# Moving GpSimd's weight sums away from the ends of third pairs, and VectorE's sums of h one step later

## The chip, the cores and the metric

The kernel runs on one core of a Trainium2 chip. The metric is the device time of one launch in microseconds (us). Every run named here is of one core; the profiled ones are all of the state "fast". Times of one kernel scatter by several us (before: 862.7 to 876.5 us over all groups of runs), so each comparison uses the runs of the kernel before that were made in the same rounds on the same chip. A ratio is the mean time of one kernel's fast runs over that of the other's fast runs of the same rounds; it is therefore not quite the ratio of the medians that are quoted beside it. One run of before in the last group (876.0 us) was marked slow and is in no ratio.

Engines in the profile: PE is TensorE (matmuls), PEld its weight loads, DVE is VectorE, ACT ScalarE, POOL GpSimd, SP SyncE. In this program the sums' operands and results lie in the memory called SBUF, TensorE's products in the one called PSUM. L207 is line 207 of the kernel. The changed kernel has nine more lines at that point, so L207 of before is L216 after.

## The reference, cut to what matters

An attention stage makes x (3072 tokens, 512 columns). Then eight experts are added up, each weighted by a routing table P that eight rounds of row and column normalisation make:

```python
for e in range(E):                         # E = 8
    h = np.maximum(x @ w1[e], 0.0)         # 512 -> 1024
    ye = h @ w2[e]                         # 1024 -> 512
    out += P[:, e:e + 1] * ye
```

## The kernel before

For experts 1 to 7 both products are done by a Strassen-like scheme with seven block products instead of eight. It needs sums and differences of quarters of all operands. Those of the weights (w1, w2) are made by GpSimd, those of h and of x by VectorE. A work item is one expert and one block of 768 tokens: there are 28. Step n of the program weaves TensorE's first product of item n (`hidden`, H) with the second product of item n-1 (`mixed`, C).

GpSimd's sums, four for each weight matrix of an expert, come from a generator of which one part runs at the end of each pair of token groups (a block has six groups of 128 tokens, taken in three pairs, i = 0, 1, 2):

```python
def quarters_of_w(e):
    ...
    pin(nc.gpsimd.tensor_tensor(s[:, 0], a21, a22, op=Alu.add))           # L139
    yield
    pin(nc.gpsimd.tensor_tensor(a21, a11, a21, op=Alu.subtract))          # L141
    yield
    pin(nc.gpsimd.tensor_tensor(s[:, 1], s[:, 0], a11, op=Alu.subtract))  # L143
    yield
    pin(nc.gpsimd.tensor_tensor(s[:, 2], a12, s[:, 1], op=Alu.subtract))  # L145
    ...
# quarters_of_w2: the same for w2, L155, L157, L159, L161

def next_weights():
    for e in range(2, E):
        for which in (1, 2):
            for half in range(2):
                load_w(e, which, pin=True, half=half)
                yield
            if which == 1:
                yield
        for g in (quarters_of_w(e), quarters_of_w2(e)):
            for n in range(4):
                next(g, None)
                if g.__name__ == "quarters_of_w" or n < 3:
                    yield
    ...
coming = next_weights()
```

VectorE's sums of h for one pair, and the places where both are called:

```python
def sums_of_h(e, b, i):
    ...
    pin(nc.vector.tensor_tensor(s_[:, 0], h21, h22, op=Alu.add))           # L206
    pin(nc.vector.tensor_tensor(s_[:, 1], s_[:, 0], h11, op=Alu.subtract)) # L207
    pin(nc.vector.tensor_tensor(h21, h11, h21, op=Alu.subtract))           # L208
    pin(nc.vector.tensor_tensor(s_[:, 2], h12, s_[:, 1], op=Alu.subtract)) # L209

ORDERS = (("a1", "d", "a2", "y", "a3", "a4", "t"), ("a1", "y", "a2", "a3", "d", "a4", "t"),
          ("a1", "a2", "y", "a3", "d", "a4", "t"))
# in mixed(e, b), for each pair i:
    for g, name in enumerate(ORDERS[i]):
        step(name)                              # one block product and its eviction
        if g == 3 and i + 1 < J // 2:
            sums_of_h(e, b, i + 1)
        if g == 6:
            if not last:
                pin(nc.gpsimd.dma_start(out=acc[:, b, i], in_=vt, accum_op=Alu.add))   # L276
            if e == E - 1 and not last:
                for j in (i, J // 2 + i):
                    pin((nc.gpsimd if final else nc.sync).dma_start(out=outv[b, j], in_=...))  # L279
            next(coming)
        ...
        yield 433

def woven(n):
    h = hidden(*work[n]) if n < len(work) else iter(())
    c = mixed(*work[n - 1]) if n else combine(B - 1)
    if n:
        sums_of_h(*work[n - 1], 0)              # the first pair's sums, at once
    ...
    parts = quarters_of_x(n + 1) if n + 1 < B else iter(())   # VectorE, only in the first blocks
    if n == 0:
        for _ in range(3):
            next(coming)
    for g, which in enumerate(plan):
        if g in (10, 19, 28, 37):
            next(parts, None)
        yield next(h if which == "H" else c)
```

So an expert has 12 places (4 blocks of 3 pairs) in which GpSimd gets one item: four loads and a pause take five, the sums the other seven, and the eighth sum shares the place of the next expert's first load. Three of the eight sums of each expert fall on the end of a third pair. Right there, `woven` asks VectorE for the next block's first sums of h.

The softmax here doesn't subtract the row's maximum and nothing guards it: scores larger than these inputs give would overflow.

Of the kernel before, what the change touches and what calls it, by code (L numbers as in the profile page):

```python
# [19 lines left out]
def kernel(  # L20
# [15 lines left out]
    E = moe_w_gate.shape[1]  # L36
# [7 lines left out]
    J = S // P  # L44
# [17 lines left out]
    def pin(ins):  # L62
        tc.keep_in_program_order(ins)
        return ins
# [41 lines left out]
    def load_w(e, which, pin=False, half=None):  # L106
        if half == 1:
            t = weights[e, which]
            src = (moe_w1[e].rearrange("(do di) f -> di do f", di=P) if which == 1
                   else moe_w2[e].rearrange("(fo fi) d -> fi fo d", fi=P))  # L110
        elif which == 1:
            t = wpool.tile([P, DO, F], F16, tag="w1")
            src = moe_w1[e].rearrange("(do di) f -> di do f", di=P)
        else:
            t = wpool.tile([P, FO, DD], F16, tag="w2")
            src = moe_w2[e].rearrange("(fo fi) d -> fi fo d", fi=P)
        part = slice(0, t.shape[1]) if half is None else slice(half * t.shape[1] // 2, (half + 1) * t.shape[1] // 2)
        ins = nc.gpsimd.dma_start(out=t[:, part], in_=src[:, part])
        if pin:
            tc.keep_in_program_order(ins)  # L120
        weights[e, which] = t
# [4 lines left out]
    def sums_of(b, j):  # L126
        if j < J // 2:
            return acc[:, b, j, 0:2, :]
        return acc[:, b, j - J // 2, 2:4, :]

    def quarters_of_w(e):

        if (e, 1) not in weights:
            load_w(e, 1, pin=True)
        t = weights[e, 1]
        lo, hi = slice(0, F // 2), slice(F // 2, F)
        a11, a12, a21, a22 = t[:, 0:2, lo], t[:, 2:4, lo], t[:, 0:2, hi], t[:, 2:4, hi]
        s = spool.tile([P, 3, 2, F // 2], F16, tag="s1")
# [7 lines that stand above are left out]
        weights[e, "q"] = dict(a11=a11, a12=a12, a22=a22, s1=s[:, 0], s2=s[:, 1], s3=a21, s4=s[:, 2])  # L146
# [16 lines left out]

    def next_weights():

        for e in range(2, E):
            for which in (1, 2):
                for half in range(2):
                    load_w(e, which, pin=True, half=half)
                    yield  # L170
                if which == 1:
                    yield
            for g in (quarters_of_w(e), quarters_of_w2(e)):
                for n in range(4):
                    next(g, None)
                    if g.__name__ == "quarters_of_w" or n < 3:
                        yield
        while True:
            yield

    coming = next_weights()

    def combine(b):
# [27 lines left out]
    def mixed(e, b):  # L211

        wq = weights[e, "t"]
        pw = pw_[-1]
        final = e == E - 1 and b == B - 1
        for i in range(J // 2):  # L216
            hq = hsums[e, b, i]
            last = final and i == J // 2 - 1
            plo, phi = pw[:, b * J + i, e:e + 1], pw[:, b * J + J // 2 + i, e:e + 1]
            if e == 1:  # L220
                for j in (i, J // 2 + i):
                    pin(nc.scalar.activation(out=sums_of(b, j), in_=sums_of(b, j), func=Act.Copy,
                                             scale=pw[:, b * J + j, 0:1]))
            a = yps.tile([P, DD // 2], F32, tag="y", name="a")
            d1 = yps.tile([P, DD // 2], F32, tag="y", name="d1")
            y2 = y2ps.tile([P, DD // 2], F32, tag="y", name="y2")
            vt = vkeep.tile([P, 4, DD // 2], F32, tag="v", name="vt")

            def prod(dst, hn, wn, first):
                for fo in range(FH):  # L230
                    pin(nc.tensor.matmul(dst, hq[hn][:, fo, :], wq[wn][:, fo, :], start=first and fo == 0,  # L231
                                         stop=fo == FH - 1, skip_group_check=True))

            def keep(k, p):
                if last and k == 1:
                    gather(k, a, p)
                    return
                pin(nc.scalar.activation(out=vt[:, k], in_=a, func=Act.Copy, scale=p))  # L238
                if last:
                    dst = acc[:, b, i, k, :]  # L240
                    pin(nc.vector.tensor_tensor(dst, dst, vt[:, k], op=Alu.add))

            def gather(k, src, p):
                dst = acc[:, b, i, k, :]
                pin(nc.vector.scalar_tensor_tensor(out=dst, in0=src, scalar=p, in1=dst, op0=Alu.mult, op1=Alu.add))  # L245

            def step(name):
                if name == "a1":
                    prod(a, "h11", "b11", True)
                    keep(0, plo)  # L250
                elif name == "a2":
                    prod(a, "s2", "t2", False)
                    keep(2, phi)
                elif name == "a3":
                    prod(a, "s1", "t1", False)
                    keep(3, phi)
                elif name == "a4":
                    prod(a, "s4", "b22", False)
                    keep(1, plo)
                elif name == "d":  # L260
                    prod(d1, "h12", "b21", True)
                    gather(0, d1, plo)
                elif name == "y":
                    prod(y2, "s3", "t3", True)
                    gather(3, y2, phi)
                else:
                    prod(y2, "h22", "t4", False)
                    gather(2, y2, phi)

            for g, name in enumerate(ORDERS[i]):  # L270
                step(name)
                if g == 3 and i + 1 < J // 2:
                    sums_of_h(e, b, i + 1)
                if g == 6:
                    if not last:
# [3 lines that stand above are left out]
                            pin((nc.gpsimd if final else nc.sync).dma_start(  # L279
                                out=outv[b, j], in_=sums_of(b, j).rearrange("p c d -> p (c d)")))  # L280
                    next(coming)
                if last and g >= 4:
                    for j, c, k, eng in {4: ((J // 2 + i, 1, 3, nc.sync), (i, 0, 0, nc.sync)),
                                         5: ((i, 1, 1, nc.scalar),), 6: ((J // 2 + i, 0, 2, nc.sync),)}[g]:
                        pin(eng.dma_start(out=outv[b, j][:, :, c * (DD // 2):(c + 1) * (DD // 2)],
                                          in_=acc[:, b, i, k, :]))
                yield 433
# [258 lines left out]
    for u in range(len(units) + 1):  # L546
        if u < len(units):
            n, h, kt = units[u]
            b, g = groups[n]
            i = u % per  # L550
# [146 lines left out]
# [4 lines that stand above are left out]
            sums_of_h(*work[n - 1], 0)  # L701
        if n == 0:
            plan = "".join("HC" if i % 7 else "H" for i in range(28))
        elif n < len(work):
            plan = "HHCHCHCHCCH" + 3 * "HHCHCHCHCHCH" + "CH"
        else:
            plan = 21 * "C"
        parts = quarters_of_x(n + 1) if n + 1 < B else iter(())
        if n == 0:
            for _ in range(3):  # L710
                next(coming)
        for g, which in enumerate(plan):
            if g in (10, 19, 28, 37):
                next(parts, None)
            yield next(h if which == "H" else c)
        assert next(h, None) is None and next(c, None) is None

    work = [(e, b) for e in range(1, E) for b in range(B)]

    def plain():  # L720
        yield from first_hidden(B - 1)
        yield from combine(B - 2)
        yield from woven(0)
# [47 lines left out]
```

## Time and profile before

| | before |
|---|---|
| median of its first three runs | 868.35 us (864.68 to 876.54) |
| span of the profiled run | 866.8 us |
| TensorE busy | 763.8 us, 88% |
| VectorE, ScalarE, GpSimd busy | 583.7, 514.9, 308.0 us |
| first h sum of the first block | 271.5 us |
| first h sum of the last block | 817.5 us |

The table of stretches shows two blocks (columns: stretch, its length, then busy time and number of instructions of PE, PEld, DVE, ACT and POOL, granted TensorE clock (1.00 is full speed), share of the DMA engines, GB/s):

```profile
579.58:600.11 20.53, 18.64 (x142) 13.59 (x141) 16.82 (x34) 12.01 (x29) 8.28 (x7) 1.00 0.63 110
600.11:618.58 18.47, 18.47 (x142) 13.68 (x141) 14.12 (x34) 12.01 (x29) 4.07 (x5) 1.00 0.84 140
```

The same 142 matmuls fill the second block completely. The first lasts 2.06 us longer, and VectorE is busy 2.7 us longer with the same 34 instructions. Most experts have three blocks of the first kind and one of the second. The groups of VectorE, with shapes kept apart, say which instructions grow (busy us, mean ns of one):

```profile
L207 DVE TENSOR_TENSOR hs<-hs,hT 128x512 f16<-128x512 f16 x84 | 79.4, 946 | 2.9
...
L208 DVE TENSOR_TENSOR hT<-hT 128x512 f16<-128x512 f16 x84 | 37.2, 443 | 0.0
L206 DVE TENSOR_TENSOR hs<-hT 128x512 f16<-128x512 f16 x84 | 37.0, 440 | 0.0
L209 DVE TENSOR_TENSOR hs<-hT,hs 128x512 f16<-128x512 f16 x84 | 34.9, 416 | 0.0
```

The other three of these four instructions of one shape and type average 416 to 443 ns. A mean twice as large may be a mixture; the view of the single line gives minimum, median and maximum, and who waited:

```profile
L207 DVE TENSOR_TENSOR hs<-hs,hT x84: 424/425/3048, 272.0 to 823.8; 128x512 f16<-128x512 f16 x84
...
  PEld L231: 39.8, 18
  PE a L231: 33.1, 18
```

Most take 425 ns, 17 of the 84 about 3,000. TensorE waits 18 times for this line: behind these 17 and once, for 0.7 us, elsewhere. (Its loads' 39.8 us and its matmuls' 33.1 us are the same waits seen twice and must not be added.) An eighteenth collision held the next line instead:

```profile
420.88 2.66 DVE L208 TENSOR_TENSOR hT<-hT 128x512 f16<-128x512 f16 x1
```

The timeline shows what the long ones stand beside (start us, length us, instruction; in brackets the idle time before it and what ended it):

```profile
579.58 0.41 DVE L206 TENSOR_TENSOR hs<-hT 128x512 f16<-128x512 f16 x1
579.74 0.85 POOL L276 DMA_DIRECT2D acc<-vt  x1 [2.43 <-ACT hT L693]
...
580.03 3.00 DVE L207 TENSOR_TENSOR hs<-hs,hT 128x512 f16<-128x512 f16 x1
...
580.34 2.39 POOL L159 TENSOR_TENSOR t<-t 128x1024 f16<-128x1024 f16 x1
...
582.95 0.41 DVE L208 TENSOR_TENSOR hT<-hT 128x512 f16<-128x512 f16 x1
...
583.09 0.61 PE L231 MATMUL a<-t,hs 128*128 128x256 f16 x4 [1.89 <-DVE hs L207]
```

L207 is recorded as running from 580.03 to 583.03 us: until 0.3 us after GpSimd's sum ends, at 582.73. TensorE stands for 1.89 us.

### The profile page before, as it was taken

To read this page: it belongs to the slowest core of one execution; us is meant where nothing else is said; L and a number is where in the kernel's file an instruction comes from. 1 tells how busy PE (TensorE), PEld (TensorE's weight loads), DVE (VectorE), ACT (ScalarE), POOL (GpSimd) and SP (SyncE) were. 2 spreads that over 40 slices of the span, in tenths; PEclk is the share of its full clock that TensorE was granted. 3 is DMA by queue.
4 is the path that set the end of the run, shared out by engine and by line. 5 is a ranking of instruction groups with operands and counts; after the bars stand their busy time and mean duration, and the time that the engine had idled before them with its cause. 6 is when DMAs were issued, how large, how long until landed. Compare 5 with 4: busy or idle time off the path is not lost.

```text
span 866.8 us, 16857 instructions
## 1 busy us (share of the span) xinstructions
PE 763.8 (88%) x6412; PEld 526.9 (61%) x6412; DVE 583.7 (67%) x1213; ACT 514.9 (59%) x1033; POOL 308.0 (36%) x323
## 2 busy tenths in 40 slices
PE   3979999999999989999999999899999999999920
PEld 1546656566555656766676666667666766677610
DVE  3435645554576797788877887887788787777720
ACT  0857776678546657765565556556565655566510
POOL 7655244556000234334424433442344244311110
PEclk9769999999899999999999999999999999999975
DMA  6965668510020733674486458436744864346663
GB/s 186 247 159 148 143 156 196 153 44 8 2 49 4 119 73 74 123 130 84 81 150 109 82 104 149 90 74 122 122 81 84 142 109 82 68 91 143 143 131 97
DMA packets 44912, 94.33 MB, mean 109 GB/s; under 512 B 10848, under 2 KB 24160, under 8 KB 44832
## 3 DMA queue, kind: packets, MB, share of 16 engines
q0 software_dynamic: 30112, 77.88, 47.0%
q1 hardware_dynamic: 13920, 14.77, 6.1%
q8 instruction: 50, 0.82, 0.4%
q10 hardware_dynamic: 800, 0.62, 0.3%
q14 instruction: 30, 0.25, 0.1%
HBM read 53.14 MB, written 7.08 MB: 69 GB/s over the span
## 4 chain that ended last, share of the span: by engine, by line
PE 68%; DVE 13%; ACT 7%; DMA 5%; issue 2%; POOL 1%; SPq 0%; ACTq 0%; POOLq 0%
PE a L231 14%; PE a L654 14%; PE d L654 9%; PE y L231 7%; PE st L449 6%; DVE hs L207 6%; ACT pt L452 4%; DVE hT L663 4%; PE hp L507 4%; PE num L465 3%; DMA acc<-vt 3%; PE yp L517 2%; PE yp L189 2%; PE d L231 2%; DVE acc L245 2%
## 5 line engine op out<-in xcount | busy, mean ns | idle before, releaser
L238 ACT ACTIVATE vt<-a,p 128x256 f32<-128x256 f32 x335 | 158.5, 473 | 193.7 <-PE a L231 193.7
L663 DVE CUSTOM_DVE_ANT_0 hT<-d,u 128x384 f16<-128x384 f32 x336 | 185.2, 552 | 101.9 <-ACT u L659 96.7
L276 POOL DMA_DIRECT2D acc<-vt x83 | 70.6, 851 | 391.7 <-ACT vt L238 168.0
L452 ACT ACTIVATE pt<-st 128x768 f16<-128x768 f32 x192 | 147.1, 809 | 73.0 <-PE st L449 72.2
L231 PE MATMUL a<-t,hs 128*128 128x256 f16 x1008 | 153.2, 275 | 35.9 <-DVE hs L207 33.1
L659 ACT COPY u<-a 128x384 f32<-128x384 f32 x336 | 160.9, 479 | 24.7 <-PE a L654 21.4
L231 PEld LDWEIGHTS <-hT 128*128 128x128 f16 x1344 | 131.3, 98 | 53.8 <-issue 2.0
L231 PEld LDWEIGHTS <-hs 128*128 128x128 f16 x1008 | 97.8, 99 | 78.1 <-DVE hs L207 39.8
L449 PE MATMUL st<-qs,ks 71*128 71x384 f16 x384 | 98.4, 339 | 17.1 <-DMA qs<-ds 12.1
L654 PE MATMUL a<-xT,s 128*128 128x384 f16 x448 | 111.2, 330 | 0.1
L654 PEld LDWEIGHTS <-t 128*128 128x128 f16 x896 | 88.0, 98 | 38.2 <-issue 2.6
L654 PE MATMUL d<-xd,t 128*128 128x384 f16 x448 | 109.4, 326 | 0.9 <-DVE hT L663 0.9
L231 PE MATMUL y<-t,hT 128*128 128x256 f16 x672 | 101.8, 274 | 1.7 <-DVE hT L208 1.1
L245 DVE SCALAR_TENSOR_TENSOR acc<-y,p,acc 128x256 f32<-128x256 f32 x168 | 80.2, 478 | 13.9 <-PE y L231 13.8
L207 DVE TENSOR_TENSOR hs<-hs,hT 128x512 f16<-128x512 f16 x84 | 79.4, 946 | 2.9
L465 PEld LDWEIGHTS <-pt 128*128 128x128 f16 x1152 | 62.9, 100 | 28.7 <-issue 4.1
L654 PEld LDWEIGHTS <-s 128*128 128x128 f16 x672 | 66.0, 98 | 17.8 <-issue 2.3
L465 PE MATMUL num<-va,pt 128*128 128x65 f16 x1152 | 68.8, 197 | 0.6 <-ACT pt L452 0.6
L361 POOL CAST t<-acc 128x768 f16<-128x768 f32 x32 | 26.3, 826 | 90.0 <-DVE acc L360 89.1
L449 PEld LDWEIGHTS <-ks 71*128 71x128 f16 x384 | 33.6, 100 | 38.4 <-issue 14.3
L693 ACT ACTIVATE hT<-a 128x384 f16<-128x384 f32 x112 | 54.1, 483 | 2.2 <-PE a L654 2.1
L654 PE MATMUL a<-xT,t 128*128 128x384 f16 x224 | 55.2, 328 | 0.0
(94 smaller groups left out, 981.2 us busy)
## 6 DMA issues: line engine op xcount, KB each, us to landing
acc<-vt POOLq DMA_DIRECT2D x83, 512.0 KB, 5.1
t<-in_moe_w_dram POOLq DMA_DIRECT2D x24, 512.0 KB, 8.2
acc<-in_k_dram POOLq DMA_DIRECT2D x7, 768.0 KB, 5.4
acc<-in_q_dram POOLq DMA_DIRECT2D x7, 768.0 KB, 5.8
v<-in_v_dram POOLq DMA_DIRECT2D x28, 192.0 KB, 4.5
out_dram<-acc SPq DMA_DIRECT2D x18, 256.0 KB
t<-in_moe_w_dram POOLq DMA_DIRECT2D x4, 1024.0 KB, 10.6
ks<-t SPq DMA_DIRECT2D x64, 48.0 KB
```

Of the source, the lines that this page charges most:

```text
L207: pin(nc.vector.tensor_tensor(s_[:, 1], s_[:, 0], h11, op=Alu.subtract))
L231: pin(nc.tensor.matmul(dst, hq[hn][:, fo, :], wq[wn][:, fo, :], start=first and fo == 0, stop=fo == FH - 1, skip_group_check=True))
L238: pin(nc.scalar.activation(out=vt[:, k], in_=a, func=Act.Copy, scale=p))
L245: pin(nc.vector.scalar_tensor_tensor(out=dst, in0=src, scalar=p, in1=dst, op0=Alu.mult, op1=Alu.add))
L276: pin(nc.gpsimd.dma_start(out=acc[:, b, i], in_=vt, accum_op=Alu.add))
L449: pin(nc.tensor.matmul(st[:, i, 0:HT], d["k"][0:KR, h, kt * P:(kt + 1) * P], d["q"][0:KR, h, i * HT:(i + 1) * HT], start=True, stop=True))
L452: pin(nc.scalar.activation(out=pt, in_=st[:, :, 0:HT], func=Act.Exp, scale=scale))
L465: pin(nc.tensor.matmul(num[:, j * (D + 1):(j + 1) * (D + 1)], pf[:, j * P:(j + 1) * P], va[:, h, kt, :], start=(kt == 0 and j == 0), stop= ...
L654: pin(nc.tensor.matmul(bk, wq[wn][:, do, f * P:(f + 1) * P], xq[xn][:, do, :], start=first and do == 0, stop=do == 1, skip_group_check=True))
L659: pin(nc.scalar.copy(t, bk))
L663: pin(add(TENSOR_ADD_SAT, out=dst, in0=bk, in1=u, s0=3e38, s1=0.0))
L693: pin(nc.scalar.activation(out=hT[:, f, hi], in_=a, func=Act.Relu))
```

## The change

The intent: give GpSimd's sums to the ends of first and second pairs only, where VectorE has no h sums due while they run, and let a third pair's h sums come one step later, so that they don't meet the GpSimd sum that now may follow a first pair.

```diff
-        for e in range(2, E):
-            for which in (1, 2):
-                for half in range(2):
-                    load_w(e, which, pin=True, half=half)
+        q1 = q2 = iter(())
+        for e in range(2, E + 1):
+            for half in range(2):
+                next(q2, None)
+                if e < E:
+                    load_w(e, 1, pin=True, half=half)
+                yield
+            for half in range(2):
+                if e < E:
+                    load_w(e, 2, pin=True, half=half)
+                yield
+                if half == 0:
+                    q1, q2 = (quarters_of_w(e), quarters_of_w2(e)) if e < E else (iter(()), iter(()))
+                    for _ in range(2):
+                        next(q1, None)
+                        yield
+            for g in (q1, q2):
+                for _ in range(2):
+                    next(g, None)
                     yield
-                if which == 1:
-                    yield
-            for g in (quarters_of_w(e), quarters_of_w2(e)):
-                for n in range(4):
-                    next(g, None)
-                    if g.__name__ == "quarters_of_w" or n < 3:
-                        yield
+                yield
...
-                if g == 3 and i + 1 < J // 2:
+                if g == 4 and i + 1 < J // 2:
                     sums_of_h(e, b, i + 1)
...
         if n == 0:
-            for _ in range(3):
+            for _ in range(2):
                 next(coming)
...
+        if n == 0:
+            next(coming)
```

No instruction is added or removed. TensorE's, ScalarE's and SyncE's orders are the same. On VectorE only the third pair's four h sums move, behind one accumulation; for the second pair, steps 3 and 4 have no VectorE instruction between them.

## The prediction

> **What bounds the kernel now.** From about 272 to 831 us run 28 steps of one token block each (18 to 25 us), bounded by TensorE: in an undisturbed block (600.11 to 618.58 us, table of stretches) it is busy in 18.47 of 18.47 us, at clock 1.00. Three of four blocks are longer: those at 559.05 and 579.58 us take 20.53 us with the same 142 matmuls. The groups view shows why: VectorE's second sum of h (hs<-hs,hT) averages 946 ns, the other three of its four sums 416 to 443; by line it is 424/425/3048 ns (min/median/max). In the timeline each long one ends when a GpSimd weight sum (2.40 us) ends: at 580.03 us the VectorE sum takes 3.00 us, the GpSimd sum runs 580.34 to 582.73. The list of waits has TensorE's weight loads waiting 18 times, 39.8 us, for these sums (matmuls 33.1 us). [...] VectorE instructions with one PSUM input keep their 0.47 and 0.55 us beside a GpSimd sum.
>
> The 18 collisions are the weight sums at the end of third pairs (3 for each of 6 experts): there the next block's first h sums are issued at once, and TensorE needs them two products later.
>
> **What changes.** Instruction counts stay; TensorE's, ScalarE's and SyncE's orders are unchanged. GpSimd's 8 sums per expert move to the 8 ends of first and second pairs; third pairs get a load or nothing. In VectorE's order only the third pair's h sums move, behind one accumulation (0.47 us). Undisturbed they would start at 609.64 us, while a GpSimd sum after the first pair would run about 607.5 to 609.9; now they start near 610.8. The next block's sums start 2.2 us after a second-pair weight sum ends. So I expect no collision in steady blocks.
>
> **Sum, all on the critical path.**
> - 17 collisions x 2.05 us (20.53 - 18.47) plus one of 1.5 (block at 420.08): -36.
> - Three were followed by 3.4 us at half clock (slow matmuls after 295, 320, 743 us; the block at 739.91 took 22.16 instead of 20.5): about 1.6 us each, -5 if the gaps cause them.
> - New: GpSimd sums now run in the first block too, where VectorE makes quarter sums of x (two SBUF inputs). Two should be held about 2 us, as at 303.83 (1.98 us) and 311.38 (2.91 us) in the second; there TensorE lost about 1.3 us: +1.5.
> - The last block's h sums come later, but the end hangs on GpSimd's serial accumulation and output transfers (from 822.83 us): +0.
>
> Sum -39.5: 868.4 -> 829 us. Range 823 to 840.
>
> **What would show it.** The second h sum's mean falls from 946 to about 430 ns, maximum below 1 us; TensorE's waits for h sums from 39.8 us to under 3; steady blocks are all near 18.5 us; VectorE's busy time falls from 583.7 to about 543 us; TensorE's stays near 760; GpSimd's sums stay 2.4 us; half-clock stretches between 270 us and the end vanish. Two quarter sums of x in the first block take about 2.5 us.
>
> **What would make it wrong.** A weight half now loads only about 10 us before its first sum (landing 8.4 us median, 11.2 at most): a late one would push GpSimd's sum into VectorE's sums of h, about 2 us for each of five experts, +10. Or the sums collide with the moved h sums after all; or half-clock stretches come back elsewhere (+5).
>
> Chances: faster by over 2% 0.96, within 2% 0.035, slower 0.005.

-36, -5, +1.5 and +0 make the -39.5.

## The result, and the profile after

| | before | after |
|---|---|---|
| median, first group of runs | 867.6 us (4 runs, the three of above among them) | 837.21 us (834.34 to 837.89, 4 runs) |
| ratio, 95% interval | | 0.9628, 0.9566 to 0.9691 |
| median, second group (other rounds) | 869.28 us (7 runs) | 833.59 us (4 runs), ratio 0.959 |
| span of the profiled run | 866.8 us | 832.5 us |
| VectorE busy / TensorE busy | 583.7 / 763.8 us | 540.0 / 755.4 us |

The change is 3.7 to 4.1% faster. The long instructions are gone. Here are the same groups of VectorE after:

```profile
L216 DVE TENSOR_TENSOR hs<-hs,hT 128x512 f16<-128x512 f16 x84 | 35.7, 425 | 2.9
L217 DVE TENSOR_TENSOR hT<-hT 128x512 f16<-128x512 f16 x84 | 35.2, 419 | 0.0
L218 DVE TENSOR_TENSOR hs<-hT,hs 128x512 f16<-128x512 f16 x84 | 35.1, 418 | 0.0
L215 DVE TENSOR_TENSOR hs<-hT 128x512 f16<-128x512 f16 x84 | 34.8, 415 | 0.0
```

So is the wait of TensorE, as the view of the single line shows:

```profile
L216 DVE TENSOR_TENSOR hs<-hs,hT x84: 424/425/428, 270.5 to 786.9; 128x512 f16<-128x512 f16 x84
...
  PEld L240: 1.1, 3
  PE a L240: 0.5, 1
```

And two blocks of the table of stretches, the second with two GpSimd sums inside it (POOL busy 7.68 us):

```profile
575.33:593.80 18.47, 18.47 (x142) 13.67 (x141) 14.11 (x34) 12.03 (x29) 7.69 (x6) 1.00 0.77 141
593.80:612.27 18.47, 18.47 (x142) 13.67 (x141) 14.12 (x34) 12.03 (x29) 7.68 (x6) 1.00 0.67 115
```

GpSimd's sums keep their length but now end before VectorE's next h sums start. In this block one runs from 601.17 to 603.61 us, and the third pair's h sums start at 604.24 us:

```profile
601.17 2.44 POOL L143 TENSOR_TENSOR s<-s,t 128x1024 f16<-128x1024 f16 x1
607.20 0.86 POOL L285 DMA_DIRECT2D acc<-vt  x1 [3.59 <-DVE hT L672]
607.80 2.41 POOL L145 TENSOR_TENSOR s<-t,s 128x1024 f16<-128x1024 f16 x1
612.43 0.86 POOL L285 DMA_DIRECT2D acc<-vt  x1 [2.22 <-DVE hT L672]
```

```profile
604.24 0.42 DVE L215 TENSOR_TENSOR hs<-hT 128x512 f16<-128x512 f16 x1
```

Where did the 34.3 us between the two profiles come from? Take the first h sum of the first and of the last block as marks (before 271.53 and 817.48 us, after 270.09 and 778.55 us):

| part | before | after | difference |
|---|---|---|---|
| up to the first block's first h sum | 271.5 | 270.1 | -1.4 |
| from there to the last block's first h sum, 27 blocks | 545.9 | 508.5 | -37.5 |
| from there to the end | 49.3 | 53.9 | +4.7 |

The blocks gained 37.5 us. One new cost is visible among them. VectorE's sums of quarters of x, which exist only in the first blocks, now meet GpSimd's sums in the first block too (timelines, before and then after):

```profile
280.81 0.55 DVE L637 TENSOR_TENSOR xT<-xT 128x768 f16<-128x768 f16 x1
...
287.61 0.55 DVE L641 TENSOR_TENSOR xd<-xT,xd 128x768 f16<-128x768 f16 x1
```

```profile
279.38 2.73 DVE L646 TENSOR_TENSOR xT<-xT 128x768 f16<-128x768 f16 x1
...
287.68 2.97 DVE L650 TENSOR_TENSOR xd<-xT,xd 128x768 f16<-128x768 f16 x1
```

The first block grew from 20.49 to 23.06 us; the second fell only from 24.76 to 21.67.

The end grew by 4.7 us. The chain that ended last is of the same kind in both profiles, an accumulating transfer of GpSimd's queue behind another (start us, length us). First before, then after:

```profile
822.83 9.52 DMA acc<-vt
...
835.00 14.07 DMA acc<-vt
```

```profile
783.90 10.41 DMA acc<-vt
...
796.97 21.15 DMA acc<-vt
```

Two profiles can't tell whether the change did this.

### The profile page after: what moved, and what is told of

Read it like the earlier page. It is cut to its first block, busy times and chain, and to the rows that moved or that the text cites. A ratio compares the mean times of both kernels' runs of the same rounds, so it can differ in the third digit from the quotient of the medians.

```text
span 832.5 us, 16856 instructions
## 1 busy us (share of the span) xinstructions
PE 755.4 (91%) x6412; PEld 525.8 (63%) x6412; DVE 540.0 (65%) x1213; ACT 515.1 (62%) x1033; POOL 309.2 (37%) x323
## 4 chain that ended last, share of the span: by engine, by line
PE 75%; DMA 10%; ACT 5%; DVE 2%; issue 2%; POOL 2%; SPq 1%; POOLq 0%; ACTq 0%; DVEq 0%
PE a L663 17%; PE a L240 16%; PE d L663 12%; PE y L240 8%; PE st L458 5%; DMA acc<-vt 4%; PE d L240 4%; PE hp L516 4%; PE yp L198 2%; PE num L474 2%; ACT pt L461 2%; DMA qs<-t 2%; PE yp L526 2%; PE hp L306 2%; ACT acc L231 2%
## 5 line engine op out<-in xcount | busy, mean ns | idle before, releaser
L240 PE MATMUL a<-t,hs 128*128 128x256 f16 x1008 | 151.2, 272 | 4.4 <-ACT vt L247 3.2
L663 PE MATMUL a<-xT,s 128*128 128x384 f16 x448 | 109.4, 326 | 0.1
L663 PE MATMUL a<-xd,s 128*128 128x384 f16 x224 | 54.3, 323 | 0.8 <-ACT u L668 0.6
```

The lines of the kernel that those rows point to most:

```text
L240: pin(nc.tensor.matmul(dst, hq[hn][:, fo, :], wq[wn][:, fo, :], start=first and fo == 0, stop=fo == FH - 1, skip_group_check=True))
L663: pin(nc.tensor.matmul(bk, wq[wn][:, do, f * P:(f + 1) * P], xq[xn][:, do, :], start=first and do == 0, stop=do == 1, skip_group_check=True))
```

## The experiments

Eleven kernels were run. Two theories stand first. **Collision theory:** a VectorE sum with two SBUF inputs is held while a GpSimd sum reads SBUF (3.00 us instead of 0.42 at 580.03 us in before); the gain is the 18 collisions. Its rivals: the later step itself relieves VectorE's queue; or any GpSimd work beside VectorE does it, whatever that work reads.

### The changed kernel again

Unchanged, for a second profile.

> The changed kernel once more, for a second profile and a comparison on one chip. Main theory (the gain is the 18 collisions between VectorE's two-input h sums and GpSimd's weight sums; what is missing from the forecast was lost at the end): ratio to before 0.962 +- 0.006, no h sum over 0.7 us, no half-clock stretch between 270 us and the end of the blocks, steady blocks 18.47 us. The span from the last block's first h sum to the end was 49.3 us in the profile of before and 54.0 us in the profile of the changed kernel. If that is chance, a second profile gives another number, anywhere in 46 to 58 us; if the change causes it, it is 53 to 55 us again.

Measured: 833.59 us against 869.28, ratio 0.959 (0.9535 to 0.9646). The blocks repeat to 0.02 us (23.07, 21.67, 19.00, 19.52, then 18.47 with a few of 18.27 to 18.76). The end took 53.1 us. This doesn't settle whether the end is the change's doing; the next runs bear on it.

### Only GpSimd's part

```diff
 # on the changed kernel
-                if g == 4 and i + 1 < J // 2:
+                if g == 3 and i + 1 < J // 2:
```

> Only GpSimd's part of the change; VectorE's h sums stay at the earlier step. Forecast's reading (the sums must go a step later, or they meet the sum after the first pair): the first h sum of a third pair starts within the last 0.3 us of a GpSimd sum and lasts 0.55 us instead of 0.42, and if TensorE waits for it, about 0.15 us is lost in 48 pairs: 7 us slower than the changed kernel. Rival (the graze is hidden, since TensorE needs that pair's sums about 3 us later): within 1 us of the changed kernel, ratio to before 0.962.

Measured: 833.62 us, ratio 0.9592, the same as the changed kernel in the same rounds (833.59). The graze (a short overlap with the tail of a GpSimd sum) is there: 20 of the 84 first h sums take 0.53 to 1.13 us, and their mean is 457 ns instead of 415. But TensorE's waits for h sums are 1.1 us in its weight loads, the same as in the changed kernel. So TensorE needs a third pair's sums later than these delays reach. The rival expectation holds: the second half of the change is worth nothing that can be measured here.

### Only VectorE's part

```diff
 # on the kernel before
-                if g == 3 and i + 1 < J // 2:
+                if g == 4 and i + 1 < J // 2:
```

> Only VectorE's part of the change; GpSimd's weight sums stay at the ends of all three pairs. Collision theory: nothing gained, because the h sums that collide are those of the first pair of a block, which do not move: ratio 1.00 +- 0.01, TensorE still waits 18 times and 35 to 42 us in its weight loads for h sums. Rival (the later step itself takes pressure off VectorE's queue): some gain, 0.99 or less. Also counts half-clock stretches: if TensorE's gaps of 2 us cause them, this profile shows 1 to 5 of them, each right after a collision; if they came by chance, they stand anywhere.

Measured: 870.72 us, ratio 1.0022 (0.9972 to 1.0071). The list of waits is that of before:

```profile
PEld L231 <- DVE hs L207: 39.8, 18, 2.8
PE a L231 <- DVE hs L207: 33.1, 18, 2.4
```

So the whole gain belongs to GpSimd's part. Two more things can be read from this profile. Its end took 53.6 us, with GpSimd's schedule of before. Eight profiles leave the transfers at the end alone: before, the two of the changed kernel, GpSimd's part, VectorE's part, and, told below, the fills and the two tries of moved x sums. Their ends are 49.3, 53.9, 53.1, 56.3, 53.6, 52.3, 58.8 and 51.6 us. A long end needs neither GpSimd's part (53.6) nor VectorE's (56.3), and the fills have neither (52.3); so nothing here charges it to the change. The profile of before, from which the prediction started, had the shortest, and it is the only one of the unchanged kernel.

The half-clock stretches came back too, in the same three blocks as before (TensorE's granted clock is 0.83 in the table of stretches, 739 to 749 us):

```profile
739.00:749.00 10.00, 7.91 (x49) 5.29 (x48) 7.53 (x14) 4.17 (x10) 2.91 (x3) 0.83 0.28 54
```

In the two profiles with collisions there are 36 gaps of TensorE of over 1 us from h sums. Behind the six longest (1.94, 2.42 and 2.09 us in before; 1.96, 2.42 and 2.09 us here) about 3.4 us at half clock follow each time; behind the other 30 (1.13 to 1.91 us) never. In the first profile of the changed kernel, which has no gap of this kind, the granted clock is 1.00 from 242 to 796 us. Taking the gaps away took the stretches away. Whether the length of the gap is what counts wasn't tested: in the clock record of before the three stretches are 3.413 us long each and start at 296.64, 320.53 and 743.78 us, so that the later two start 23.9 and 447.1 us after the first, 7 and 131 times that length. Each of the three gaps before them lies inside one step of that grid, and of the other 15 of this profile only 6 do (the longest 1.90 us). The place of a gap would fit as well as its length.

### Fills instead of sums

The order of before, but where GpSimd would have added at the end of third pairs it fills, which writes SBUF and reads none. Its output is wrong, which doesn't matter for the time.

```diff
 # on the kernel before; the same for s[:, 2] (the last FILL elements) and for t[:, 0]; FILL = 2700
-        pin(nc.gpsimd.tensor_tensor(s[:, 0], a21, a22, op=Alu.add))
+        if e == 1:
+            pin(nc.gpsimd.tensor_tensor(s[:, 0], a21, a22, op=Alu.add))
+        else:
+            pin(nc.gpsimd.memset(s.rearrange("p a b c -> p (a b c)")[:, 0:FILL], 0.01))
```

> The kernel before, with its order kept, but the three weight sums of each expert from the second on that end third pairs are replaced by fills of 2,700 fp16 elements per partition (about 2.4 us), which only write SBUF; the result is wrong on purpose. Theory[...] (a two-input VectorE sum is held only by a GpSimd instruction that reads SBUF): no h sum at the head of a block is held, 18.5 us steady blocks, ratio 0.955 to 0.97, close to the changed kernel, although GpSimd is busy at the very same places. Rival (any GpSimd work beside it, or its writes to SBUF, holds VectorE): h sums of 2.5 to 3 us stay, ratio 0.99 to 1.01.

Measured: 832.81 us, ratio 0.9589 (0.9531 to 0.9646). In the timeline GpSimd's fill, somewhat longer than the sum that it replaces, stands at the head of the block, and VectorE runs straight through it:

```profile
462.69 0.42 DVE L217 TENSOR_TENSOR hs<-hs,hT 128x512 f16<-128x512 f16 x1
463.04 0.42 DVE L218 TENSOR_TENSOR hT<-hT 128x512 f16<-128x512 f16 x1
463.37 0.42 DVE L219 TENSOR_TENSOR hs<-hT,hs 128x512 f16<-128x512 f16 x1
```

```profile
462.98 2.63 POOL L152 MEMSET s<- 128x2700 f16 x1
```

It is not GpSimd's being busy, nor its writing, that holds VectorE. What is left is its reading; a fill is also another kind of instruction, and no run tests a GpSimd instruction that only reads. That the reading decides is therefore theory, and this run agrees with it: 0.42 us beside a fill, 3.00 us beside a sum. This kernel also has no new collision in the first block, which takes 20.50 us (20.49 in before).

### The quarter sums of x elsewhere

```diff
 # on the changed kernel
-            if g in (10, 19, 28, 37):
+            if g in (4, 10, 27, 42):
```

> The changed kernel, with VectorE's quarter sums of x in each block moved to other places of the plan (4, 10, 27, 42 in place of 10, 19, 28, 37), so that none should run beside a GpSimd weight sum. Theory (what the forecast undersized is the new hold on these sums in the first block: it lost 2.6 us there, not 1.5): the first two blocks fall from 23.06 and 21.67 us to 20.5 and 19 to 20.5, no quarter sum of x above 0.7 us, 3 to 4.5 us less than the changed kernel, 829 to 831 us where that takes 833.6. Rival (they are long because VectorE's own queue is full in these blocks): they stay above 22 and 21 us in sum, within 1 us of the changed kernel.

Measured: 831.3 us against 868.54, ratio 0.957; changed kernel 0.959 in other rounds, so that in the whole time no gain is clear of noise. The first two blocks took 20.89 and 19.62 us, 4.2 us less together; the third rose by 0.3. Four of the sums still met a GpSimd sum, in part (0.91 and 1.81 us in the first block, 0.80 and 1.63 in the second), though none above 0.7 was expected. The cause holds: of the 2.57 us by which the first block had grown, 2.17 came back.

A second try took the places 4, 10, 30 and 46:

> The changed kernel with the quarter sums of x at places 4, 10, 30, 46: in the first try two of them still met a GpSimd sum (0.91 and 1.81 us instead of 0.55). Theory: all quarter sums of x take 0.55 us, the first two blocks together fall from 44.7 us (changed kernel) to 40 us or less (they took 40.52 in the first try); the time falls with them, to within its spread of some 3 us: 829 to 832 us.

All quarter sums of x now take 0.55 us, but the two blocks are at 20.89 and 19.79 us, no better. "40 us or less" was a miss: the rest of their length isn't this collision. Time: 831.21 us against 871.22, ratio 0.9552.

### The last block added up by VectorE

```diff
 # on the changed kernel
-            last = final and i == J // 2 - 1
+            last = final
```

> The changed kernel, with all three pairs of the last block added up by VectorE and written out in quarters at once, as the last pair is already; no accumulating DMA in the last block. In all six profiles 49 to 56 us pass from the last block's first h sum to the end, while TensorE is done about 13 us after it: the end waits for accumulating transfers (9.5 to 21 us each in the two first profiles). Theory (the end is GpSimd's serial chain of accumulation, wait, output): 8 to 20 us less. Rival (the end is the backlog of output transfers on SyncE's queue, issues of which take 4 to 7 us there): less than 4 us gained, or a loss.

Measured: 830.87 us against 868.54, ratio 0.9565; with the first try of moved x sums as well:

> Both together: if the two are independent, the sum of the two gains within 2 us.

829.42 us, ratio 0.9548. By the ratios, with 0.959 for the changed kernel in other rounds, the gains are about 1.7 us (moved x sums), 2.2 us (last block) and 3.7 us (both): estimates within the noise, additive as expected. The 8 us expected of the last block didn't come; "less than 4 us", the rival, is what was measured. In the chain that ended last in the first of these two runs, the accumulations are replaced by SyncE's queue and a wait for its output transfers:

```profile
782.95 4.98 SPq L288
...
792.31 4.39 SPq L288
...
799.41 14.46 DMA out_dram<-acc
```

The trace of the changed kernel shows how this builds up. SyncE's issue of one 256 KB output takes 0.5 us at 746 us and 7.0 us at 783 us. With the last block on VectorE (830.87 us), ScalarE, which has to issue a quarter of that block's output itself, ends one activation at 782.94 us and its next one only some 20 us later, and VectorE waits 17.92 us for ScalarE:

```profile
803.63 0.42 DVE L250 TENSOR_TENSOR acc<-acc,vt 128x256 f32<-128x256 f32 x1 [17.92 <-ACT vt L247]
```

### The outputs of the last expert on GpSimd's queue

In the last expert GpSimd has no sums left to make. Both kernels build on the second try of moved x sums.

```diff
 # at g == 6, after the accumulating transfer; the first run gave only j >= J // 2 to GpSimd
+                    if e == E - 1:
+                        for pb, pj in owed_outs:
+                            pin(nc.gpsimd.dma_start(out=outv[pb, pj], in_=sums_of(pb, pj)...))
+                        owed_outs.clear()
                     if e == E - 1 and not last:
                         for j in (i, J // 2 + i):
-                            pin((nc.gpsimd if final else nc.sync).dma_start(out=outv[b, j], in_=...))
+                            owed_outs.append((b, j))
```

> The same, and of the two output transfers of each pair of the last expert one goes to GpSimd's queue, one pair later, when its accumulation has landed. In the profiles SyncE's issues of these transfers grow from 0.5 us to 4 to 7 us from the second block of the last expert on, and its last one goes out 35 us after the last block begins: a backlog. Theory (the backlog is SyncE's queue alone): SyncE's issues stay under 1 us and the end comes 8 to 20 us sooner. Rival (the DMA engines, or the memory behind them, are what is full): the transfers take as much longer on GpSimd's queue, and less than 4 us is gained.

> The same, with both transfers on GpSimd's queue one pair later; SyncE issues only the last pair's quarters. Theory of SyncE's queue: as the one with half, or better. Rival: no gain, since accumulations and outputs then stand in one queue, or the engines are full.

Measured in the same rounds: 831.21 us with all on SyncE but the last block's, 825.65 us with half on each (ratio 0.9493), 818.0 us with all on GpSimd (ratio 0.94, 0.9364 to 0.9437). With half on each, the 5.6 us gained lie between the theory's 8 and the rival's 4: that expectation was missed. From the last block's first h sum to the end it is now 51.6, 50.2 and 42.5 us. The full move is the better one by far, which points to SyncE's queue rather than to the DMA engines alone. It isn't shown: the outputs also go out one pair later here, and no run moved them later without moving them over. What makes that queue slow stays open too.

The two accumulations of the last block are now all the long pieces that are left in the chain (10.18 and 16.99 us). So the two parts were joined:

> The kernel with both outputs of the last expert on GpSimd's queue, and the last block added up by VectorE and written out in quarters, without accumulating DMA. Alone, the second part gained little, because ScalarE and SyncE stood behind the backlog of outputs; without the backlog, what is left of the end is the two accumulations of the last block, 10 and 17 us one after the other in the last profile. Theory: these fall away, 8 to 18 us less than 818.0 us. Rival (the quarters on SyncE's and ScalarE's queues meet the GpSimd queue's last transfers and ScalarE is held again): within 4 us of 818, or slower.

Measured: 813.36 us (809.64 to 816.84), against 871.42; ratio 0.9352, 0.9306 to 0.9399. Its end takes 33.9 us. The gain over the previous kernel, 4.6 us of medians in different rounds, is less than the 8 us expected: ScalarE stands still for 3.2 and 3.5 us, since its own output issue in the last block waits for VectorE. This version is right and beats both kernels of the change.

## Why the prediction was right or wrong

- **The mechanism: right.** The h sums' second instruction fell from 946 to 425 ns on average (about 430 was said), its maximum from 3,048 to 428 ns, TensorE's waits from 39.8 to 1.1 us, VectorE's busy time to 540.0 us (543 was said), and steady blocks to 18.47 us; two x sums of the first block rose to 2.73 and 2.97 us (about 2.5 was said). GpSimd's part alone gives the whole gain, and the fills show that GpSimd's being busy or writing isn't enough.
- **The sum for the blocks: nearly right.** 36 us for collisions, 5 for half-clock stretches, less 1.5 for the x sums, makes 39.5. The blocks gave 37.5. The differences of steady blocks are the 2.05 us that were used, and the three half-clock stretches went away.
- **The term that was mis-sized: "there TensorE lost about 1.3 us: +1.5".** The first block grew by 2.57 us, and the second fell 0.56 us less than the other two terms say (24.76 - 2.05 - 1.6 is 21.11; it took 21.67). That is +3.1, twice the term. The mistake was to read the cost of a hold from TensorE's waits in a block that was slow already. TensorE's idle time (a block's length less its busy time) rose from 0.83 to 2.53 us in the first block; in the second, the 1.94 us gap behind the h sum set aside, from 1.36 to 2.26 us: part of what these holds cost had been hidden there. About 0.5 us of the +3.1 isn't accounted for by this. In the first try of moved x sums the idle time is back at 0.84 and 0.75 us.
- **"+0" for the end.** In the profile it was +4.7 us. Nothing charges it to the change: each half alone, and the fills with neither, have a long end too. The prediction took the end of one profile (49.3 us) as fixed, where eight profiles have 49 to 59. That, the x sums and the scatter between groups of runs are enough for 834 to 837 us instead of 829; no run splits the rest between them. The time lay inside the range, in its upper half.
- **The h sums one step later.** The prediction read the overlap in time rightly (609.64 us against a GpSimd sum until 609.9) and let it stand as a reason for the second half of the change. The grazes do happen without it, but no one waits: 833.62 against 833.59 us.
- **The feared late loads** didn't come: a half's landing takes 7.6 us (median of the 24 loads after 230 us), and no GpSimd sum waits for one.

## What to carry to other kernels

When one of several instructions of the same shape has twice the mean of the others, look at its minimum and maximum, then at what GpSimd does beside the long ones: in these traces a VectorE instruction with two SBUF inputs beside a GpSimd sum ended 0.3 to 0.4 us after that sum, and TensorE, which needed the result, stood for up to 2.42 us. The recorded start doesn't tell who is held: in all 21 holds of over 0.6 us in the profile of before it is VectorE, in 18 of them although its record starts first (by 0.08 to 0.33 us; at 580.03 us against 580.34), while the GpSimd sums beside them kept their 2.39 to 2.42 us. Why was not shown. Here the cure was to move GpSimd's work to places where VectorE's next few instructions take one of their two tensors from PSUM (those kept their 0.47 and 0.55 us beside a sum). Check every other instruction with two SBUF inputs for the new places too. A hold cost time here only where someone needed the result before it ended: 20 grazed sums cost nothing, 18 others cost up to 2 us each.
